# Attention and MLP on one core: where the projection steps, the shared tiles and the pauses stand in a hand-written order

## The chip, the core and the metric

One core of a Trainium2 chip runs the whole kernel. The metric is the device time of one execution in microseconds (us); the number compared is the median over several runs. TensorE is called PE (its weight loads PEld), VectorE DVE, ScalarE ACT, GpSimd POOL, SyncE SP.

## The reference

Eight batches, eight heads, 576 positions, head size 64. Attention keeps only scores within tau of each row's maximum; its output, 4608 rows of 512, goes through two dense layers with g = h - tanh(h) between them.

```python
scores = scale * np.matmul(q, k.transpose(0, 1, 3, 2))
thresh = np.max(scores, axis=-1, keepdims=True) - tau
scores = np.where(scores >= thresh, scores, -1000000000.0)
scores = scores - np.max(scores, axis=-1, keepdims=True)
attn = np.exp(scores)
attn = attn / (np.sum(attn, axis=-1, keepdims=True) + 1e-09)
attn_out = np.matmul(attn, v)
...
x = attn_out.transpose(0, 2, 1, 3).reshape(B * S, H * D)
h = x @ w_in            # 512 -> 2048
g = h - np.tanh(h)
out = g @ w_out         # 2048 -> 512
```

## The kernel before

The order of all instructions is written out by hand; no scheduler moves them. Every engine works through its own instructions in that order and waits only for what it needs.

**Tiles.** Two heads of one batch make a pair; there are 32 pairs p, four per batch. The 576 query rows of two heads are nine tiles of 128 rows: four of each head, and one shared tile that holds the last 64 rows of both. `place(i)` puts the shared tile last in an even pair and first in an odd pair, so the shared tiles of pairs 0 and 1, 2 and 3 and so on are neighbours in the list of 288 tiles. `kind(i)` is "A" for even and "B" for odd tile numbers; an A and the B behind it share some work (one `nb`, one transpose, one attention output).

**One tile.** `scores` multiplies q with the high and low parts of k into a PSUM tile psS of the pool ps_big, which has two buffers: four matmuls on line L331 for a whole tile (512, 64, 512 and 64 columns), eight matmuls with 64 output rows each on line L322 for a shared tile. DVE takes psS out to sc with the row maximum (L341). `shift` makes the bias nb (L353), `kink` lets ACT make z (L368), and z is transposed: by PE (L387) in pairs 0 to 5, by a DMA that SP issues (zT, L375) in the later pairs. `weights` lets ACT take the exponential pT (L396 or L404). `attend` multiplies pT with v (L425, L432, L443), `norm` divides, and `emit_x` transposes a finished pair into xT through psX in the pool ps_h.

**The loop.** Step s of the main loop issues the scores of tile s + 8, z of tile s + 5, the exponential of tile s, and attention of tile s - 2 (in the first 36 tiles the last two come earlier). It also runs what `plan` has for it: loads, the split of q and k on POOL, and `turn`, which transposes k (and some q) on PE through a ps_big buffer, copies it out on DVE (L263) and swaps its halves on POOL (kS, L269). For pairs from 5 on, `turn` of k comes in step 9p - 14 for odd p and 9p - 11 for even p. In one step the order is: shift, scores, kink, tanh of earlier hidden steps, weights, projection and hidden steps, shrink, stores, attend, plan.

**The dense layers.** Stage m handles 512 rows of batch m (the rest of all batches is stage 8). `layers(m)` gives a list of steps of two kinds. A hidden step is four 512-column matmuls into psH of the pool ps_h (L498, two buffers, shared with psX); ACT takes tanh (L511) and DVE makes g (L517) in the next loop step. A projection step is a quarter of a 128-row output: four 512-column matmuls into psY (L524; one buffer, pool ps_y). The fourth quarter is copied out by DVE to yo (L537) and stored by SP (L540). A stage has 16 hidden steps and 16 projection steps. Since a projection needs g, only the first `EARLY(m)` projection steps of block m are in its own stage; the others come in stage m + 1, mixed with that stage's hidden steps. In stage 0 projection waits for all 16 hidden steps.

Stage m starts at step 36(m + 1) + 4, when its x is there. `share` is the number of steps handed out per loop step: the list is spread over 32 loop steps and is finished four steps before the next stage starts. So in each 36 steps there are four without dense work. Stage 7 starts after the last tile and, with stage 8, makes up the tail.

Of the kernel before, what the change touches and what calls it, by code (L numbers as in the profile page):

```python
# [18 lines left out]
def kernel(  # L19
# [14 lines left out]
    B, H, S, D = q.shape  # L34
# [11 lines left out]
    HPAIR = H // 2  # L46
    NPAIR = B * HPAIR
# [4 lines left out]
    TPP = 9  # L52
    NTILE = NPAIR * TPP
# [9 lines left out]
    AHEAD = 8  # L63
    LDK = 16
    MASK = 5
    LAG = 2
# [177 lines left out]
    def q_by_dma(p):  # L244

        return p >= 2 * HPAIR and p % 4 != 0
# [51 lines left out]
    def kind(i):  # L298

        return "AB"[i % 2]  # L300

    def place(i):

        p, j = divmod(i, TPP)
        j = j - p % 2
        return (p, None, 4) if j in (-1, 8) else (p, j // 4, j % 4)

    def scores(i):
        p, hh, t = place(i)
        qT, kT, kS = mats[p, "q"], mats[p, "k"], mats[p, "ks"]  # L310
        ps = ps_big.tile([P, 1024], F32, name="psS", tag="big")
        main, rem, lo = slice(0, 512), slice(512, 576), 0
        if kind(i) == "B":
            main, rem, lo = slice(512, 1024), slice(448, 512), 448
        if hh is None:
            qrem = REM
            if q_by_dma(p):
                qrem = (slice(512, 640, 2), slice(513, 640, 2))
            for n, kk in enumerate((kT, kS)):
                for dst, srcs in ((main, MAIN), (rem, REM)):  # L320
                    for hh in range(2):
                        nc.tensor.matmul(  # L322
                            out=ps[64 * hh : 64 * hh + 64, dst],
                            lhsT=qT[:, qrem[hh]], rhs=kk[:, srcs[hh]],
                            start=(n == 0), stop=(n == 1),
                        )
        else:
            lhs = qT[:, (5 * hh + t) * P : (5 * hh + t + 1) * P]
            for n, kk in enumerate((kT, kS)):
                for dst, src in ((main, MAIN[hh]), (rem, REM[hh])):  # L330
                    nc.tensor.matmul(  # L331
                        out=ps[:, dst], lhsT=lhs, rhs=kk[:, src],
                        start=(n == 0), stop=(n == 1),
                    )
        sc = sc_pool.tile([P, S], F32, name="sc")
        if kind(i) == "B":
            mx = mxs[i] = mxs.pop(i - 1)
        else:
            mx = mxs[i] = mx3[i // 2 % len(mx3)]
        c = int(kind(i) == "B")  # L340
        nc.vector.tensor_scalar(  # L341
            out=sc, in0=ps[:, lo : lo + S], scalar1=SC, scalar2=None,
            op0=ALU.mult, op1=ALU.max, accum_out=mx[:, c : c + 1],
        )
        scs[i] = sc
# [148 lines left out]
    def hidden(m, n, ps):  # L494
        if n == 0:
            gs[m] = g_pool.tile([P, DF_C, MB], BF16, name="g")
        for c in range(DM_C):
            nc.tensor.matmul(  # L498
                out=ps, lhsT=w_in_sb[:, c, n * P : (n + 1) * P],
                rhs=xs[m][:, c, :] if m < B else xR[:, c, :, :],  # L500
                start=(c == 0), stop=(c == DM_C - 1),
            )
        halves.append((m, n, ps))
# [3 lines left out]
    def bend():  # L507
        while halves:
            m, n, ps = halves.pop(0)
            th = t_pool.tile([P, MB], F32, name="th")  # L510
            nc.scalar.activation(out=th, in_=ps, func=ACT.Tanh)  # L511
            ths.append((m, n, ps, th))
# [37 lines left out]
                    )  # L550


    EARLY = lambda m: 3 if m else 3
    LAST = 1

    FIRST = 3
# [2 lines left out]
    def layers(m, tail):  # L559


        def h_step(n):
            if tail and n % 2:
                ps = ps_big.tile([P, MB], F32, name="psHt", tag="big")
            else:
                ps = ps_h.tile([P, MB], F32, name="psH", tag="h")
            hidden(m, n, ps)

        def y_step(m, ms, part):
            if part == 0:  # L570

                odd = tail and (m, ms) > (B - 2, 1) and ms % 2 == 0
                pl, tag = (ps_o, "o") if odd else (ps_y, "y")
                ys[m, ms] = pl.tile([P, d_model], F32, name="psY", tag=tag), odd
            ps, odd = ys[m, ms]
            project(m, ms, part, ps, odd)

        def y_half(h):

            n = d_model // 2  # L580
            pl, tag = ((ps_y, "y"), (ps_o, "o"))[h]
            ps = pl.tile([P, n], F32, name="psY", tag=tag)
            for part in range(4):
                project(m, 3, part, ps, h == 0, slice(h * n, h * n + n))

        now = quarters(m - 1)[EARLY(m - 1) :] if m > 0 else []
        if m < NMB - 1:
            now += quarters(m)[: EARLY(m)]
        else:
            now += quarters(m)[:12]  # L590
        n = 16 + len(now)


        ahead = n - max(0, EARLY(m) - 3) - LAST if m < NMB - 1 else n - 9 - LAST
        steps, at, i = [], [], 0

        def ready(y):
            last = 4 * y[2] + 3
            return y[0] < m or len(at) > (last if m else 15) and at[last] + 2 < i

        while now or len(at) < 16:
            if len(at) < 16 and (
                not now or not ready(now[0]) or len(at) * ahead <= i * 16
            ) and not (m == B - 1 and i < FIRST):
                steps.append(lambda a=len(at): h_step(a))
                at.append(i)
            elif ready(now[0]):
                steps.append(lambda y=now.pop(0): y_step(*y))
            else:
                steps.append(lambda: None)  # L610
            i += 1
        if m == NMB - 1:
            steps += [lambda h=h: y_half(h) for h in range(2)]
        return steps
# [15 lines left out]
    def w_cast():  # L630
        flat, wt, i, cols = loaded.pop(0)
        nc.gpsimd.tensor_copy(out=flat[:, i * cols : (i + 1) * cols], in_=wt)
# [26 lines left out]
    for p in range(1, NPAIR):  # L659
        first = TPP * p - AHEAD  # L660
        for d, f in PREP[3 if p == 1 else 0 :]:
            d -= p == 1 and d in (3, 5)
            if d in (7, 8) and q_by_dma(p):
                d = d + 2
            if p in (2, 4):
                d = {8: 9, 7: 8, 5: 6}.get(d, d)
            elif d == 5 and p >= 5:
                d = 6 if p % 2 else 3
            plan.setdefault(first - d, []).append(lambda p=p, f=f: f(p))
        d = 7 if q_by_dma(p) else 3 - (p == 1 or p >= 5)  # L670
        d = 4 if p in (2, 4) else d
# [16 lines left out]
    todo, stage = [], 0  # L688
# [4 lines left out]
            plan.setdefault(-AHEAD, []).extend(plan.pop(at))  # L693


    kinks, wts, atts = {}, {}, {}
    for i in range(NTILE + 3):
        at = i - 4 if i < HPAIR * TPP else i
# [4 lines left out]
    for s in range(-AHEAD, NTILE + LAG + 3):  # L703
        p, j = divmod(max(s, 0), TPP)
        if 0 <= s < NTILE and j == 2 + LAG and p % HPAIR == 0 and p >= HPAIR:
            assert not todo
            todo = layers(stage, False)
            share = len(todo) / (HPAIR * TPP - 2 - LAG)
            done, stage = 0.0, stage + 1
        if s == NTILE:  # L710
            todo = layers(stage, True)
            share, done, stage = 1, 0.0, stage + 1
        if 0 <= s + AHEAD - 1 < NTILE:
            shift(s + AHEAD - 1)
        if 0 <= s + AHEAD < NTILE:
            scores(s + AHEAD)
        if s == 1 - AHEAD:
            for t in ("k", "q", "ks"):
                turn_first(t, 1)
        for i in kinks.pop(s, []):  # L720
            kink(i)
        bend()
        for i in wts.pop(s, []):
            weights(i)
        if 0 <= s < NTILE + FIRST:
            if todo:
                done += share
                if s < NTILE and j == TPP - 1 and p % HPAIR == HPAIR - 1:
                    done = 1e9
                while todo and done >= 1:  # L730
                    todo.pop(0)()
                    done -= 1
        if s == 0:
            nc.vector.tensor_tensor(
                out=fold, in0=ident_bf[:, 0:64], in1=ident_bf[:, 64:P], op=ALU.add
            )
        shrink()
        for store in stores[:-1]:
            store()
        del stores[:-1]  # L740
        for i in atts.pop(s, []):
            pp, jj = divmod(i, TPP)
            if i < NTILE:
                attend(i)
                odd = pp % 2
                if jj == 3 + odd:
                    norm(pp, 0)
                elif odd and jj in (0, 8):
                    norm(pp - (jj == 0), 1)
            if pp and jj == 1 + pp % 2:  # L750
                emit_x(pp - 1)
        for step in plan.pop(s, []):
            step()
        if s + AHEAD in cast_when:
            w_cast()
        if s + AHEAD in load_when:
            w_load(next(pieces))
# [54 lines left out]
```

## Time and profile before

| | |
|---|---|
| median of five runs | 533.52 us (532.0 to 535.44) |
| the profiled execution | 532.75 us, span 530.9 us |
| granted TensorE clock | 0.998 |
| busy, share of the span | PE 96%, ACT 82%, DVE 79%, POOL 55%, PEld 54% |
| PE instructions | 4606 matmuls, 4606 weight loads |
| projection matmuls (L524) | 592, 145.9 us |
| hidden matmuls (L498, into psH) | 480, 123.3 us |
| score matmuls of whole tiles (L331), with kT and with kS | 512 and 496, 104.4 and 101.3 us |
| eviction of scores (L341, DVE) | 288, mean 752 ns |
| exponential of a pair of tiles (L404, ACT) | 117, mean 1154 ns |

The chain of work that ended last is PE for 44% of the span, "issue" 16%, POOL 15%, ACT 11% and DVE 8%. Times of groups are busy times; a matmul's end is modelled, and neighbours overlap. "Idle before" is time in which the engine stood still just ahead of a group, with what ended it. The steps of the loop can be found in the trace by counting psS tiles: those of step s are tile s + 8.

### The profile page before, as it was taken

The page shows a single profiled execution, that of the slowest core. Times are in us where ns is not written, and L with a number is a line of the kernel's source. Part 1 is how long each engine was busy: PE and PEld are TensorE (multiplying, and loading weights), DVE is VectorE, ACT ScalarE, POOL GpSimd, SP SyncE. Part 2 cuts the span into 40 slices and gives each one's busy share as a digit, 9 for nine tenths or more (in the row PEclk, how much of TensorE's full clock was granted, in tenths as well). Part 3 has the DMA queues.
Part 4 walks back from the last instruction along what each step waited for, and adds up shares of the span by engine and source line. Part 5 has one row for each costly group of instructions (what it writes and reads, how often), then busy time and mean ns, then how long its engine had stood idle before and what let it go on. Part 6 is the DMA issues. An engine that isn't in the chain of part 4 may idle for free.

```text
span 530.9 us, 12716 instructions
## 1 busy us (share of the span) xinstructions
PE 507.8 (96%) x4606; PEld 287.5 (54%) x4606; DVE 420.9 (79%) x1179; ACT 434.6 (82%) x617; POOL 289.9 (55%) x390
## 2 busy tenths in 40 slices
PE   8999899988999999999999999999999999999996
PEld 4666566554555555555555555655555555444444
DVE  5899879997889988898889988898889887554440
ACT  5999899979898979899898989898989999544330
POOL 7999989684736657575727574665757530000000
PEclk9999999999999999999999999999999999999999
DMA  7843659989988999799998999899999996400113
GB/s 204 255 139 111 215 187 189 169 151 203 177 205 160 182 183 214 168 184 211 171 199 179 199 180 203 172 189 197 203 173 182 205 146 110 105 36 26 38 41 80
DMA packets 208607, 86.79 MB, mean 163 GB/s; under 512 B 176160, under 2 KB 200992, under 8 KB 208544
## 3 DMA queue, kind: packets, MB, share of 16 engines
q1 hardware_dynamic: 207952, 85.56, 76.1%
q8 instruction: 36, 0.59, 0.5%
q10 hardware_dynamic: 592, 0.43, 0.3%
q14 instruction: 27, 0.22, 0.1%
HBM read 36.70 MB, written 9.44 MB: 87 GB/s over the span
## 4 chain that ended last, share of the span: by engine, by line
PE 44%; issue 16%; POOL 15%; ACT 11%; DVE 8%; DMA 4%; SPq 1%; POOLq 0%; ACTq 0%; DVEq 0%
PE psY L524 14%; PE psH L498 11%; PE psS L331 8%; ACT z L368 5%; POOL kS L269 5%; ACT pT L396 3%; DMA zT<-z 3%; DVE sc L341 3%; PE psHt L498 3%; PE psO L432 2%; POOL khl L193 2%; ACT pT L404 2%; PE psS L322 2%; ACT th L511 2%; DVE g L517 2%
## 5 line engine op out<-in xcount | busy, mean ns | idle before, releaser
L341 DVE TENSOR_SCALAR_CACHE_REDUCE sc<-psS 128x576 f32<-128x576 f32 x288 | 214.0, 752 | 38.2 <-PE psS L331 24.9
L368 ACT ACTIVATE z<-sc,nb 128x576 bf16<-128x576 f32 x288 | 215.4, 769 | 19.8 <-DVE nb L353 17.9
L404 ACT ACTIVATE pT<-zT 128x1152 f16<-128x1152 bf16 x117 | 135.0, 1154 | 15.9 <-DMA zT<-z 15.9
L524 PE MATMUL psY<-w_out_sb,g 128*128 128x512 bf16 (+1 forms) x592 | 145.9, 373 | 0.8 <-DVE yo L537 0.8
L269 POOL COPY kS<-kT 64x1152 f16<-64x1152 f16 x62 | 70.9, 1143 | 122.0 <-DVE nb L353 120.4
L498 PE MATMUL psH<-xT,w_in_sb 128*128 128x512 bf16 x480 | 123.3, 379 | 3.5 <-DVE g L517 3.5
L331 PEld LDWEIGHTS <-qT 128*128 128x128 f16 x1024 | 74.5, 97 | 61.7 <-issue 7.5
L331 PE MATMUL psS<-kT,qT 128*128 128x512 f16 (+1 forms) x512 | 104.4, 285 | 3.2 <-DVE sc L341 1.5
L517 DVE SCALAR_TENSOR_TENSOR g<-th,psH 128x512 bf16<-128x512 f32 x128 | 87.5, 684 | 21.3 <-ACT th L511 20.9
L331 PE MATMUL psS<-kS,qT 128*128 128x512 f16 x496 | 101.3, 286 | 1.9 <-POOL kS L269 1.9
L511 ACT ACTIVATE th<-psH 128x512 f32<-128x512 f32 x128 | 74.7, 584 | 22.3 <-PE psH L498 21.8
L524 PEld LDWEIGHTS <-g 128*128 128x128 bf16 x592 | 51.0, 98 | 56.8 <-issue 2.4
L498 PEld LDWEIGHTS <-w_in_sb 128*128 128x128 bf16 x576 | 49.3, 98 | 58.5 <-issue 6.0
L432 PE MATMUL psO<-vb,pT 128*128 128x65 bf16 x1024 | 53.3, 194 | 0.0
L432 PEld LDWEIGHTS <-pT 128*128 128x128 f16 x1024 | 44.2, 98 | 9.7
L193 POOL TENSOR_TENSOR qhl<-qraw,qhl 128x576 f16<-128x576 f32 x31 | 39.7, 1281 | 2.6
L193 POOL TENSOR_TENSOR khl<-kraw,khl 128x576 f16<-128x576 f32 x31 | 39.7, 1280 | 2.6
L396 ACT ACTIVATE pT<-psZ 128x512 f16<-128x512 bf16 (+1 forms) x54 | 35.1, 654 | 3.3 <-PE psZ L387 3.1
L537 DVE COPY yo<-psY 128x512 f32<-128x512 f32 (+1 forms) x31 | 21.1, 682 | 14.1 <-PE psY L524 12.4
L425 PE MATMUL psO<-vb,pT 128*128 128x130 bf16 x128 | 28.2, 221 | 3.4 <-ACT pT L404 2.7
L458 DVE TENSOR_TENSOR osb<-psO,rc 128x256 bf16<-128x256 f32 x64 | 27.2, 424 | 2.2
L263 DVE COPY kT<-ps_k 128x1152 f16<-128x1152 f16 x31 | 23.3, 751 | 3.9 <-PE ps_k L240 3.9
(79 smaller groups left out, 508.9 us busy)
## 6 DMA issues: line engine op xcount, KB each, us to landing
vraw<-in_v_dram SPq DMA_DIRECT2D x32, 256.0 KB, 4.0
out_dram<-yo SPq DMA_DIRECT2D x32, 256.0 KB, 2.8
kraw<-in_k_dram SPq DMA_DIRECT2D x31, 256.0 KB, 3.4
qraw<-in_q_dram SPq DMA_DIRECT2D x31, 256.0 KB, 3.5
wt<-in_moe_w_in_dram SPq DMA_DIRECT2D x8, 512.0 KB, 4.9
wt<-in_moe_w_out_dram SPq DMA_DIRECT2D x8, 512.0 KB, 4.0
zT<-z SPq DMA_TRANSPOSE x117, 3.6
qraw<-in_q_dram SPq DMA_DIRECT2D x32, 32.0 KB, 3.5
```

The lines of the kernel that those rows point to most:

```text
L193: nc.gpsimd.tensor_tensor(out=hl[:, :, 1, :], in0=x, in1=hl[:, :, 0, :], op=ALU.subtract)
L269: nc.gpsimd.tensor_copy(out=o, in_=i)
L331: nc.tensor.matmul(out=ps[:, dst], lhsT=lhs, rhs=kk[:, src], start=(n == 0), stop=(n == 1),)
L341: nc.vector.tensor_scalar(out=sc, in0=ps[:, lo : lo + S], scalar1=SC, scalar2=None, op0=ALU.mult, op1=ALU.max, accum_out=mx[:, c : c + 1],)
L368: nc.scalar.activation(out=z, in_=sc, func=ACT.Prelu, bias=nb, scale=1.0, alpha=STEEP)
L396: nc.scalar.activation(out=pt[:, off * P : (off + n) * P], in_=ps[:, 0 : n * P], func=ACT.Exp)
L404: nc.scalar.activation(out=pt[:, 0 : n * P], in_=zts.pop(i)[:, 0:n, :], func=ACT.Exp)
L432: nc.tensor.matmul(out=po[:, t - 1 + ab, :], lhsT=pt[:, blk * P : (blk + 1) * P], rhs=vb[:, hh, c, :], start=False, stop=(n == 7), skip_gr ...
L498: nc.tensor.matmul(out=ps, lhsT=w_in_sb[:, c, n * P : (n + 1) * P], rhs=xs[m][:, c, :] if m < B else xR[:, c, :, :], start=(c == 0), stop= ...
L511: nc.scalar.activation(out=th, in_=ps, func=ACT.Tanh)
L517: nc.vector.scalar_tensor_tensor(out=gs[m][:, n, :], in0=th, scalar=-1.0, in1=ps, op0=ALU.mult, op1=ALU.add,)
L524: nc.tensor.matmul(out=ps, lhsT=gs[m][:, n, ms * P : (ms + 1) * P], rhs=w_out_sb[:, n, cols], start=(n == 0), stop=(n == DF_C - 1),)
```

## The change

Four things are changed, all of them in the order of the instructions; PE's instructions are the same 4606 matmuls as before, in another order.

- `EARLY(m)` is max(3, 9 - m) instead of 3. Stage 0 has 16 hidden and 9 projection steps (before 16 and 3), stages 1 to 6 have 16 and 15 (before 16 and 16), stages 7 and 8 are as before.
- In `layers`, `ahead` follows `EARLY`: hidden steps come earlier in their stage, and in stage 0 one with each step until all 16 are out.
- The list of a stage is spread over all steps up to the start of the next stage, except those in which `turn` of a k is planned (`turns`). Stage 6, the last one within the tiles, is spread over its last 32 loop steps as before.
- The scores of a shared tile of kind A are held back by one step and issued right ahead of those of the shared tile of kind B.

```diff
-    EARLY = lambda m: 3 if m else 3
+    EARLY = lambda m: max(3, 9 - m)
...
         ahead = n - max(0, EARLY(m) - 3) - LAST if m < NMB - 1 else n - 9 - LAST
+        if m == 0:
+            ahead = 16
...
+    turns = set()
+    for p in range(HPAIR + 1, NPAIR):
+        d = 6 if p % 2 else 3
+        turns.add(TPP * p - AHEAD - (d if p >= 5 else 5))
...
-            share = len(todo) / (HPAIR * TPP - 2 - LAG)
+            room = range(s, min(s + HPAIR * TPP, NTILE))
+            if room[-1] + 1 < NTILE:
+                room = [a for a in room if a not in turns]
+            share = len(todo) / len(room)
...
-        if 0 <= s + AHEAD < NTILE:
-            scores(s + AHEAD)
+        n = s + AHEAD
+        if 0 < n < NTILE and place(n)[1] is None and kind(n) == "B":
+            scores(n - 1)
+        if 0 <= n < NTILE and (place(n)[1] is not None or kind(n) == "B"):
+            scores(n)
...
-            if todo:
+            if todo and (s >= NTILE or s in room):
                 done += share
-                if s < NTILE and j == TPP - 1 and p % HPAIR == HPAIR - 1:
+                if s < NTILE and s == room[-1]:
```

## The prediction

> **What bounds the kernel now.** I read the page's busy shares and its 40 slices first, then busy time stage by stage, then the order of time on TensorE, then the waits.
>
> ```profile
> PE 507.8 (96%) x4606; PEld 287.5 (54%) x4606; DVE 420.9 (79%) x1179; ACT 434.6 (82%) x617; POOL 289.9 (55%) x390
> ...
> PE   8999899988999999999999999999999999999996
> DMA  7843659989988999799998999899999996400113
> ```
>
> PE is at nine tenths or more nearly everywhere from the tenth slice on; a shared average would hide that the first quarter is different. So I cut the span where the hidden layer of each block starts (matmul psS of step s = 40, 76, 112, ..., 256):
>
> ```profile
> core 0: us, PE busy (x) PEld busy (x) DVE busy (x) ACT busy (x) POOL busy (x), PEclk, DMA share, GB/s
> 65.06:121.52 56.46, 51.21 (x550) 31.65 (x548) 48.57 (x141) 50.66 (x77) 46.50 (x58) 1.00 0.83 180
> 121.52:179.15 57.63, 56.70 (x521) 31.73 (x519) 50.00 (x142) 52.01 (x72) 33.46 (x44) 1.00 0.93 184
> 352.81:410.00 57.19, 56.39 (x522) 31.67 (x520) 50.29 (x144) 52.01 (x72) 34.43 (x45) 1.00 0.96 190
> 410.00:447.73 37.73, 37.10 (x325) 20.17 (x323) 32.69 (x93) 34.95 (x49) 12.81 (x17) 1.00 0.85 155
> ```
>
> The first row is stage 0, the next ones stage 1, stage 5 and the start of stage 6. Stages 1 to 5 take 57.63, 58.23, 57.76, 57.67 and 57.19 us, 288.48 together. A PE matmul's end is modelled, so I count starts instead: in the trace a 512-column matmul follows the last after 0.216 us, a 65-column one after 0.03 us, a transpose after 0.055 us. Time beyond such distances is PE standing still: 2.0, 2.6, 2.2, 2.1 and 1.6 us in stages 1 to 5 (10.4 in all), 7.4 in stage 0, 1.0 from 410.00 to 447.73. So stages 1 to 5 are 55.6 us of PE work each and PE is their bound; ACT, next, has 52 us. Stage 0 has only 56.46 - 7.4 = 49.1 us of PE work: it isn't bound by PE, and PE's largest halt lies there:
>
> ```profile
> 111.95 0.42 PE L432 MATMUL psO<-vb,pT 128*128 128x65 bf16 x8
> 112.21 0.41 PE L331 MATMUL psS<-kT,qT 128*128 128x512 f16 x2
> ...
> 117.88 0.41 PE L331 MATMUL psS<-kS,qT 128*128 128x512 f16 x2
> 120.95 0.23 PE L425 MATMUL psO<-vb,pT 128*128 128x130 bf16 x1 [2.66 <-ACT pT L404]
> ```
>
> In the four tiles without projection before s = 76, PE runs ahead and then waits 2.66 us for an exponential. The same tiles of a later stage:
>
> ```profile
> 175.84 0.41 PE L322 MATMUL psS<-kS,qT 128*64 128x512 f16 x4
> 176.08 0.42 PE L322 MATMUL psS<-kT,qT 128*64 128x512 f16 x4
> ...
> 177.35 0.41 PE L331 MATMUL psS<-kS,qT 128*128 128x512 f16 x2
> 177.79 0.41 PE L331 MATMUL psS<-kT,qT 128*128 128x512 f16 x2
> 178.03 0.41 PE L331 MATMUL psS<-kS,qT 128*128 128x512 f16 x2
> 178.58 0.23 PE L425 MATMUL psO<-vb,pT 128*128 128x130 bf16 x1
> ```
>
> 0.44 and 0.55 where 0.24 would do, and a third such place: 0.6 us of standing per stage, since evictions and exponentials can't follow at 0.9 us a tile.
>
> **Part 1, nine projection steps in stage 0.** Six steps leave stages 1 to 6, one each, and join stage 0. A step is four matmuls; the lines below give 144.78 - 143.92 = 0.86 us. Stages 1 to 5 lose 5 x 0.86 = 4.3 us, stage 6 0.86. Stage 0 gains 5.2 us of PE work: 49.1 + 5.2 = 54.3, above ACT's 50.66, so it turns PE-bound. With the standing of a PE-bound stage (1.6 to 2.6) it would take 56 to 57; with all 7.4 kept, 61.7. I take 3.1, nearer the PE-bound rows because the 2.66 us halt is in the very tiles that now get four projection steps (3.4 us): 57.4, so +0.9 (bounds -0.5 and +5.2). The moved steps also bring two yo copies (0.69 us of DVE each) and two stores into stage 0; DVE has 48.57 of 56.46 there; a store's issue takes SP some 0.55 us, ahead of the zT issues queued behind it, which land up to 4 us before ACT wants them. I count both at nothing; uncovered, the copies would cost 1.4 us and the issues 1.1. All 16 hidden steps of stage 0 now come in s = 41 to 63 (14 there before): 2 x 0.58 of tanh and 2 x 0.68 of g move earlier, inside the +0.9.
>
> **Part 2, joined shared tiles.** A shared tile uses matmuls of 64 output rows (L322):
>
> ```profile
> 143.92 1.03 PE L524 MATMUL psY<-w_out_sb,g 128*128 128x512 bf16 x4
> 144.78 0.22 PE L425 MATMUL psO<-vb,pT 128*128 128x130 bf16 x1
> 144.84 0.41 PE L432 MATMUL psO<-vb,pT 128*128 128x65 bf16 x8
> 145.18 0.44 PE L322 MATMUL psS<-kT,qT 128*64 128x512 f16 x4
> 145.45 0.42 PE L322 MATMUL psS<-kS,qT 128*64 128x512 f16 x4
> 145.80 1.04 PE L498 MATMUL psH<-xT,w_in_sb 128*128 128x512 bf16 x4
> ```
>
> Eight 65-column matmuls take 0.34 us before an L322 (144.84 to 145.18) and 0.26 before an L331 (111.95 to 112.21); the last L322 before a full one takes 0.35 (145.45 to 145.80), before another L322 0.24 (175.84 to 176.08). A visit thus costs 0.08 + 0.11 = 0.19 us. In the order of PE's instructions there are 25 visits before and 16 after. Where two shared tiles fell in tiles without projection they already stood together; so the nine that go are three before s = 40, where ACT sets the pace (56.49 of 65.06 us busy; I count 0, at most 0.6), and one in each of stages 1 to 6: 5 x 0.19 = 1.0 and 0.2. The joined step puts two evictions (752 ns each) in a row on DVE; behind them wait yo and the g of the step before, 0.75 us later. The score buffers are two and both were freed a step earlier, and the step before has no eviction; I count 0.
>
> **Part 3, even spread.** Steps now fill the four empty tiles, and each stage's four steps that transpose a k (turn) get none. The 0.6 us per stage in the empty tiles goes: 3.0 over stages 1 to 5. What is late next: ps_h has two buffers, and a hidden step needs the g of the one before last. Where a psX lies between two hidden steps in neighbouring tiles, that g comes only after this step's eviction, 0.75 + 0.68 us. By the schedule's order this happens twice, at s = 58 and 94 (bounds 0 and 1.5 each; I take 1.1 for s = 94, and s = 58 is in stage 0's +0.9); before, milder forms of it stood three times a stage. Together I put the standing of stages 1 to 5 at 8.5 instead of 10.4: -1.9 (bounds -6.4, 0.8 a stage, and 0).
>
> One rule of the Trainium skill speaks against parts 1 and 3: Perfetto Trace Analysis, Identifying the Most-Contended Engine, holds busy matmul time to be a bad measure for TensorE and asks for the weight loads' share, which is 54% here. By it TensorE has room to spare, moving its work would shorten nothing, and the sum would be 0. The starts, 216 ns apart with 2 us of standing in 57.7, decide against it here.
>
> **Sum.** Stages 1 to 5: -4.3 - 1.0 - 1.9 = -7.2; stage 6: -1.05; stage 0: +0.9; before s = 40 and after 447.73 (same steps): 0. That is -7.3. The profiled execution took 532.75 (its span is 530.9), so 525.4 on its scale; the median of the runs is 0.77 above it: 533.5 - 7.3 = 526.2.
>
> **Rivals.** (a) *Stage 0 does not hide the steps.* Its halts come from latencies (exponentials, g) that the new work only pushes on: +5.2 instead of +0.9, so -3.0: 530.5. For it: ACT and DVE are also at 50.7 and 48.6 there. Against it: 2.66 of 7.4 us is one halt that the steps fill.
>
> (b) *The transposes by DMA hold the stages.*
>
> ```profile
> ACT pT L404 <- DMA zT<-z: 11.9, 8, 2.4
> ```
>
> From 121.52 to 410 ACT waits 11.9 us for zT, and DMA is at 0.93 to 0.96. If that paces the stages they can't get below the shortest one: 5 x 57.19 - 288.48 = -2.5; stage 6 gives nothing, stage 0 +0.9: -1.6, so 531.9. Against it: these waits hardly reach PE (2.2 us for pT in the same stretch), and even spacing takes away the bursts that cause some of them.
>
> (c) *Slower: the turn steps lose their cover.* There are 24 (four in each of stages 0 to 5). PE needs 2.71 us for one with a projection and psX (s = 85), 1.85 without it; DVE's eviction, g, xT, xR and kT copy take 2.4 by their starts. Where no psX lies, 1.3 against 1.95. If the next scores wait for the kT copy every time, that is 24 x 0.6 = 14.4 us: 533.5 - 7.3 + 14.4 = 540.6. It decides from (7.3 + 2.7) / 24 = 0.42 us a turn step. Against it: DVE has only 50.4 of 57.7 us, the next step gives it 1.65 us for one eviction, and the second buffer gives the copy one more step.
>
> (d) That the change doesn't do what it says is excluded: the order shows 16 visits, and nine projection steps before the next stage's first hidden step.
>
> **Numbers.** Forecast 0.70; (a) 0.12; (b) 0.11; (c) 0.07. The forecast's own range: down by 4.5 (standing), 1.4 (stage 0) and 0.6, not all at once: 520.5; up by 1.9 and 1.6: 529.7. With (a), and (b) up to its centre: 520.5 to 532.0; (c), half of (b) and the tails are left out. About 0.5% (2.7 us) is what a measurement of this kernel can tell from no change. Faster: nearly all of the forecast and half of (a), 0.75; same: most of (b), half of (a), 0.16; slower 0.09.
>
> **What would show it.** Right: stages 1 to 5 near 56.2 each; stage 0 near 57.4 with no halt of over 1 us before s = 76; 16 visits of L322; PE standing near 1.7 a stage. (a): stage 0 over 60. (b): stages over 57 with ACT waiting for zT. (c): PE standing for kT or sc in the step behind each turn. The prediction is wrong if stages 1 to 5 stay above 57.5, or fall below 55.

## The result and the profile after

The changed kernel takes 532.33 us (median of 46 runs, 530.94 to 535.96), the kernel before 533.69 (86 runs). The ratio is 0.9978, interval 0.997 to 0.9987: 1.2 us faster, where 7.3 were forecast. It lies just above the range's upper end of 532.0.

The profiled execution took 533.72 us, with a span of 531.9. That is 1.4 above the median of its kernel, while the one of before was 0.9 below its own; the two executions therefore differ by +1.0 where the medians differ by -1.4. So whatever rests on a difference of 1 us between two profiles is shown by timed kernels below, not by the profiles alone.

The busy shares on the changed kernel's page:

```profile
PE 507.7 (95%) x4606; PEld 286.2 (54%) x4606; DVE 419.0 (79%) x1179; ACT 434.7 (82%) x617; POOL 289.3 (54%) x390
```

Nothing has moved here, and nothing could: the work is the same. Busy time by stage, cut at the same loop steps as before (length first, then the engines):

```profile
64.56:122.40 57.84, 55.53 (x574) 33.58 (x572) 50.39 (x143) 51.24 (x77) 47.89 (x60) 1.00 0.81 179
122.40:181.90 59.50, 56.64 (x518) 31.34 (x515) 49.87 (x143) 53.83 (x73) 34.41 (x45) 1.00 0.94 186
...
355.27:411.68 56.41, 55.58 (x517) 31.20 (x515) 49.06 (x143) 50.69 (x69) 34.33 (x44) 1.00 0.97 185
411.68:448.29 36.61, 36.17 (x320) 19.80 (x318) 31.76 (x93) 33.89 (x47) 10.90 (x13) 1.00 0.90 156
```

Stage 0 is 57.84 (forecast 57.4), the start of stage 6 is 1.12 shorter (forecast 1.05). Stages 1 to 5 are 59.50, 57.15, 57.49, 58.73 and 56.41: 289.3 together, where 281.3 were forecast and 288.5 stood before. PE's work in them, by the distances of the starts, is 272.5 instead of 278.05: the forecast 5 x (0.86 + 0.19) = 5.25 is there. What isn't there is the time: PE stands still for 16.8 us instead of 10.4. By the matmul that stood still:

| stages 1 to 5, us | before | changed |
|---|---|---|
| scores (psS) in the 3 us behind a turn, and the turn itself (ps_k) | 0.9 | 8.0 |
| projection, waiting for yo (psY) | 0 | 2.1 |
| psX, waiting for g | 0 | 1.75 |
| hidden step, waiting for g (psH) | 4.1 | 1.8 |
| scores elsewhere, attention (psO) | 3.05 | 1.0 |
| second half of the scores, waiting for kS | 2.4 | 2.2 |

Of the 8.0 us, 4.6 stand within 1 us of a turn: 3.5 at the ten turns of even pairs, 1.1 at the ten of odd pairs, whose steps also hold a psX. Before the change these were 0.

A turn step of an even pair in the changed kernel, PE in the order of time (start, duration, operation, idle time before it), and below it the two evictions of DVE in the same stretch:

```profile
243.42 0.41 PE L331 MATMUL psS<-kT,qT 128*128 128x512 f16 x2
243.67 0.41 PE L331 MATMUL psS<-kS,qT 128*128 128x512 f16 x2
243.94 0.22 PE L425 MATMUL psO<-vb,pT 128*128 128x130 bf16 x1
244.00 0.41 PE L432 MATMUL psO<-vb,pT 128*128 128x65 bf16 x8
244.59 0.66 PE L240 MATMUL ps_k<-ident_f,khl 128*128 128x128 f16 x9 [0.18 <-DVE sc L341]
245.26 0.41 PE L331 MATMUL psS<-kT,qT 128*128 128x512 f16 x2
```

```profile
243.78 0.75 DVE L341 TENSOR_SCALAR_CACHE_REDUCE sc<-psS 128x576 f32<-128x576 f32 x1
...
244.45 0.75 DVE L341 TENSOR_SCALAR_CACHE_REDUCE sc<-psS 128x576 f32<-128x576 f32 x1
```

The transposes begin 0.59 us after the 65-column matmuls where 0.26 would do, and the next scores 0.67 after the transposes where 9 x 0.055 = 0.5 would do. Both wait for sc: they start 0.06 us after the first and the second eviction have ended (244.53 and 245.20). ps_big has two buffers, and turn takes one: between these scores and the next ones that want the same buffer PE now has only the attention and the transposes, about 0.8 us, and DVE needs 0.75 for the eviction alone, behind whatever it was doing. A dense step of 0.86 us used to stand between them. The prediction's 1.3 us of PE work where no psX lies is there (1.84 from 243.42 to 245.26, less 0.5 of standing); its hope for "one more step" was not fulfilled, since the wait is for the eviction too, not only for the copy of kT. PE standing for sc at the turns is also the sign that the prediction had named for its rival (c).

### The profile page after: what moved, and what is told of

Read it like the earlier page. It is cut to its first block, busy times and chain, and to the rows that moved or that the text cites. A ratio compares the mean times of both kernels' runs of the same rounds, so it can differ in the third digit from the quotient of the medians.

```text
span 531.9 us, 12676 instructions
## 1 busy us (share of the span) xinstructions
PE 507.7 (95%) x4606; PEld 286.2 (54%) x4606; DVE 419.0 (79%) x1179; ACT 434.7 (82%) x617; POOL 289.3 (54%) x390
## 4 chain that ended last, share of the span: by engine, by line
PE 43%; DVE 14%; issue 12%; ACT 11%; POOL 9%; DMA 9%; SPq 0%; ACTq 0%; POOLq 0%; DVEq 0%
PE psY L524 13%; PE psH L498 12%; PE psS L331 9%; DMA zT<-z 7%; DVE sc L341 5%; ACT z L368 4%; DVE g L517 3%; POOL kS L269 3%; ACT pT L396 3%; PE psHt L498 3%; ACT pT L404 2%; PE psO L432 2%; ACT th L511 2%; DMA vraw<-in_v_dram 2%; DVE kT L263 1%
## 5 line engine op out<-in xcount | busy, mean ns | idle before, releaser
L368 ACT ACTIVATE z<-sc,nb 128x576 bf16<-128x576 f32 x288 | 218.5, 769 | 21.3 <-DVE nb L353 20.5
```

What stands on the lines that cost most here:

```text
L368: nc.scalar.activation(out=z, in_=sc, func=ACT.Prelu, bias=nb, scale=1.0, alpha=STEEP)
```

## The experiments

Seventeen kernels, all timed beside the kernel before (533 to 534 us in each set; 0.5% is 2.7 us). Kernels of different sets are compared by their medians; by their ratios to the kernel before, a difference can come out up to 1.4 us apart, so where the two disagree both are given. Where a profile lacks some matmul records (62 to 68 of 4606), the distance that a missing one leaves is not counted as standing.

**Fill the turn steps.** The one line that keeps them empty goes:

```diff
             room = range(s, min(s + HPAIR * TPP, NTILE))
-            if room[-1] + 1 < NTILE:
-                room = [a for a in room if a not in turns]
```

> The change, but the turn steps get dense steps too (spread over all 36 loop steps of a stage). Theory 1 (uncovered turns): in the changed kernel PE stands 8.0 us in stages 1 to 5 between a turn and the scores behind it, or ahead of the turn, against 0.9 before; with a dense step in front of each turn that falls to 2 at most and the time to 526 to 528 us. Theory 2 (the denser hidden steps make DVE late everywhere): the standing moves to other places and the time stays within 531 to 534.

Measured: 526.05, ratio 0.9845 (0.9819 to 0.9871). This is the time that the prediction gave for the change. A turn step of that kernel:

```profile
240.41 0.41 PE L331 MATMUL psS<-kS,qT 128*128 128x512 f16 x2
240.65 1.03 PE L498 MATMUL psH<-xT,w_in_sb 128*128 128x512 bf16 x4
241.52 0.22 PE L425 MATMUL psO<-vb,pT 128*128 128x130 bf16 x1
241.57 0.41 PE L432 MATMUL psO<-vb,pT 128*128 128x65 bf16 x8
241.83 0.66 PE L240 MATMUL ps_k<-ident_f,khl 128*128 128x128 f16 x9
242.38 0.41 PE L331 MATMUL psS<-kT,qT 128*128 128x512 f16 x2
```

0.26 and 0.55: no halt. The standing at the turns of stages 1 to 5 falls from 8.0 to 2.9 (2 at most were expected), all standing there from 16.8 to 11.1. Theory 1 holds for this kernel, theory 2 doesn't.

**The old spread, and each part alone.**

```diff
-            room = range(s, min(s + HPAIR * TPP, NTILE))  # and without turns
+            room = range(s, s + HPAIR * TPP - 2 - LAG)
```

> The change with the old spread (32 loop steps in a row, four empty ones), so early projection steps and joined shared tiles alone. Theory 1: PE work of stages 1 to 6 falls by 1.05 us each, standing stays as before, stage 0 grows by 1.4: 533.7 - 6.3 + 1.4 = 528.8, range 528 to 530.5. Theory 2: the hidden steps come as densely as in the change, so 532 or more.

Measured: 534.02, ratio 1.0008 (0.9992 to 1.0024). A miss for theory 1, and within what theory 2 said.

> The kernel before with the early projection steps alone. Theory 1: 6 x 0.86 us less work in stages 1 to 6, stage 0 longer by 1.4: 533.7 - 3.8 = 529.9, range 529 to 531.5. Theory 2: 533 or more. Rival (a) of the prediction: stage 0 grows by all 5.2, so 533.7.

Measured: 535.0, ratio 1.0026 (1.0008 to 1.0043). The early steps alone make the kernel slower, as theory 2 said. Stage 0 takes 59.43 us, 3.0 more than before, and its largest halt is one that the prediction never looked for (PE in the order of time):

```profile
107.92 0.60 PE L524 MATMUL psY<-w_out_sb,g 128*128 128x512 bf16 x2
109.97 0.59 PE L524 MATMUL psY<-w_out_sb,g 128*128 128x512 bf16 x2 [1.45 <-POOL w_out_sb L634]
```

The first projection steps overtake POOL's cast of w_out. In the changed kernel projection begins at 105.3 us instead of 100.9, and this halt isn't seen. PE's work in stages 1 to 5 fell by 4.3 as computed; standing rose from 10.4 to 13.6.

> The kernel before with the even spread alone (turn steps and no others left empty). Theory 1: some 7 us of standing at the turns of stages 1 to 5 come in, 2 to 3 us in the four empty tiles of each stage go: 536 to 539. Theory 2: with the old sparse hidden steps the spread costs nothing and saves the empty tiles' standing: 530 to 533.

Measured: 534.99, ratio 1.0022 (1.0006 to 1.0039). Slower, by less than theory 1 said; neither range was met. PE stands 7.9 us at the turns of stages 1 to 5 instead of 0.9, and most of the standing at empty tiles and psH went.

So the early steps alone and the spread alone each cost a little over 1 us, the early steps with the joined tiles in the old spread change nothing that can be told from noise, and the three together gain 1.2 us. The joined tiles alone were not run.

**Which part does the filled kernel need?**

> The change with dense steps in the turn steps too, but without the joined shared tiles. By 0.19 us for a visit: with dense steps between them none of the neighbouring shared tiles of stages 0 to 6 stands together any more, so 13 joints take a second visit, 2.5 us: 528 to 529 against 526.05 of the kernel with the join. Rival: the join's double eviction costs as much as the visits save: 526.

Measured: 525.98, ratio 0.9855 (0.983 to 0.9881): no difference, the rival's number. In its profile PE works 2.1 us more in stages 1 to 5, as the further visits ask, and stands 7.6 us instead of 11.1; that it is the double evictions which cost this was not tested by itself.

> The change with dense steps in the turn steps too, but with three early projection steps in every stage as before. If the early steps are worth what the sum said once the turns are covered (6 x 0.86 less work, stage 0 longer by 1.4): 526.05 + 3.8 = 529.9, range 529 to 531. Rival: they are worth nothing, as in the kernel with the early steps alone, and the gain is all the spread's: 525 to 527.

Measured: 526.33, ratio 0.9863 (0.9839 to 0.9888): no difference either.

> The kernel before with its dense steps spread over all 36 loop steps of a stage, and nothing else changed. If the early steps and the joined tiles are worth nothing once there are no empty steps, as the two runs without one of them say: 525.5 to 527. If each of them only covers for the other: 528 to 530.

Measured: 528.78, ratio 0.9919 (0.9901 to 0.9938). Both together are worth 2.7 us by the medians, 3.9 by the ratios (the intervals don't meet); a spread without empty steps is worth 4.2 by itself. Beside the spread with empty turn steps alone (534.99) that is 6.2 us: the empty turn steps have the same price here as in the changed kernel (532.33 against 526.05).

> Dense steps in the turn steps too, and six yo copies on ACT in place of DVE: those after which the next dense step opens psY again at once. PE stood 2.1 us in stages 1 to 5 and 0.45 in stage 0 for these copies in the filled kernel. If ACT is free there (no tanh is left in these steps): 524 to 525. Rival: ACT is late itself and the exponentials behind the copy are pushed on by 0.6 us each: 526 or more.

Measured: 527.1, ratio 0.9879 (0.9855 to 0.9902): no gain, the rival's number. The halts for yo were not cured but grew: in its profile psY stands 3.7 us in stages 1 to 5 instead of 2.1, and 2.4 in stage 0, where the longest halt is for ACT's copy. Whether late exponentials add to it was not looked into.

**Does it matter where the empty steps are?**

```diff
-        turns.add(TPP * p - AHEAD - (d if p >= 5 else 5))
+        turns.add(TPP * p - AHEAD - (d if p >= 5 else 5) + 4)
```

> The change, but the four empty steps of a stage stand four steps behind each turn of k instead of in it. Theory 1 (the turn step needs a dense step in front of the turn): the 8.0 us of standing go and 526 to 528 is reached as in the filled kernel. Theory 2 (31 dense steps in 32 places instead of 36 are too close together, wherever the gaps are): 531 to 533.

Measured: 531.92, ratio 0.9968 (0.9946 to 0.999). A miss for theory 1 as it stood, and within theory 2's range: the standing at the turns did go (8.0 to 1.7), but 5.2 us ahead of psX came in its place. In this one execution the longest of these halts (2.05 us) is followed by 3.4 us at a granted clock of 0.50, with matmuls twice as far apart; other runs at a clock of 1.0 took up to 533.45, so the clock is not what keeps this kernel slow.

> The change with only two empty steps in a stage, those of the turns of odd pairs. If every empty step costs the same wherever it stands (6.3 us for 24 of them, 0.26 us each): 12 steps, 529.2. If the cost comes from the turns of even pairs, where 0.2 to 0.5 us of standing was seen at nearly each of them: 527.

Measured: 526.85, ratio 0.9886 (0.9864 to 0.9907). With empty steps at the odd pairs' turns alone most of the cost is gone: by the medians 0.8 of 6.3 us is left, by the ratios 2.2 of 7.1. Half would have been left if each empty step cost the same, a ratio of 0.9911 and just outside the interval. It fits the trace of the changed kernel, where the halts next to a turn lie at the even pairs (3.5 us against 1.1).

**The second cause: SP's queue.** Where did the 5.2 us ahead of psX come from? A milder form of the same wait stands in the filled kernel (first the order of time on ACT, then on SP, whose rows are DMA issues, then a row of DVE and one of PE):

```profile
294.98 0.76 ACT L368 ACTIVATE z<-sc,nb 128x576 bf16<-128x576 f32 x1
...
304.43 1.17 ACT L404 ACTIVATE pT<-zT 128x1152 f16<-128x1152 bf16 x1 [1.81 <-DMA zT<-z]
305.50 0.76 ACT L368 ACTIVATE z<-sc,nb 128x576 bf16<-128x576 f32 x1
306.17 0.57 ACT L511 ACTIVATE th<-psH 128x512 f32<-128x512 f32 x1
```

```profile
295.63 1.57 SPq L375 DMA_TRANSPOSE zT<-z  x1
297.24 0.61 SPq L145 DMA_DIRECT2D qraw<-in_q_dram  x1
297.90 0.57 SPq L153 DMA_DIRECT2D qraw<-in_q_dram  x1
298.51 0.59 SPq L145 DMA_DIRECT2D vraw<-in_v_dram  x1
299.14 1.73 SPq L151 DMA_DIRECT2D vraw<-in_v_dram  x1
300.97 2.76 SPq L375 DMA_TRANSPOSE zT<-z  x2
```

```profile
306.78 0.69 DVE L517 SCALAR_TENSOR_TENSOR g<-th,psH 128x512 bf16<-128x512 f32 x1 [1.25 <-ACT th L511]
```

```profile
307.52 0.38 PE L475 MATMUL psX<-ident_bf,osb 128*128 128x128 bf16 x4 [1.23 <-DVE g L517]
```

The z of one pair of tiles was ready at 295.74, but SP issued its transpose only at 300.97, behind another transpose and four loads. ACT stood 1.81 us for it; behind that stood a tanh, behind the tanh a g, and behind the g PE, 1.4 us ahead of psX by the starts. SP issues without a pause from 295.63 to 303.73. For these 8 us the trace is the second case in the Trainium skill's Perfetto Trace Analysis, What "DMA-bound" means: an issuing engine's track that is solid with DMA slices. It is so in bursts only: in stages 1 to 5 of this kernel SP waits 117 us for ACT. The remedy that the page names for this case, large descriptors, was not tried; the loads were set apart instead:

```diff
-        (LDK - 1, lambda p: load(p, "q")),
-        (LDK - 2, lambda p: load(p, "v")),
+        (LDK - 2, lambda p: load(p, "q")),
+        (LDK - 5, lambda p: load(p, "v")),
```

> All three parts, no empty steps, and the loads of q and v of a pair set one and three steps later, so that SP doesn't issue four loads between two transposes. Theory D (SP's queue and the DMA behind it hold the exponentials now; ACT waited 10.6 us for zT in stages 1 to 5 of the filled kernel, one z lay 5.2 us before SP came to it): the wait falls below 6 us and the time to 523 to 525. Rival (these waits are absorbed before they reach PE): 526, whatever ACT waits.

Measured: 521.84, ratio 0.9788 (0.9769 to 0.9807). The fastest kernel of the study, 11 us under the kernel before and below what was expected. In the waits of the whole span, first of the filled kernel, then of this one (total, times, longest):

```profile
ACT pT L404 <- DMA zT<-z: 15.0, 17, 2.3
```

```profile
ACT pT L404 <- DMA zT<-z: 3.5, 8, 0.8
```

PE's standing in stages 1 to 5 is 7.1 us. The DMA share there is 1.01, not lower than in the changed kernel (0.94 to 1.00), so the order in the queue changed and not the load on the DMA engines.

> As the kernel with the loads set apart, but with three early projection steps in every stage. Theory D: with SP out of the way PE is the bound again, so the early steps are worth 2 to 4 us: 526 to 528 here. Rival: still worth nothing, within 1 us of the kernel with them.

Measured: 523.36, ratio 0.9817 (0.9798 to 0.9836). The early steps are worth 1.5 us here, less than expected. The intervals of the two ratios overlap, but the kernels were timed side by side, and each run of this one (522.9 to 523.6) is above each run with the early steps (521.4 to 522.1). Stages 2 to 5 of its profile take 55.65, 55.65, 55.75 and 55.65 us: PE-bound, with 0.3 to 0.4 us of standing.

> The kernel before, with nothing but these loads set later. Theory D: most of the 4.1 us that PE stood for psH in stages 1 to 5 came from late exponentials, so 529 to 531. Rival: PE had the cover for it, 532 to 533.5.

Measured: 529.46, ratio 0.9933 (0.9917 to 0.9948). The kernel before gains 3.6 us from this alone. The number is theory D's, the place is not: psH in stages 1 to 5 falls only from 4.1 to 2.4, and these stages together by 1.2 us (288.48 to 287.24). The larger part is stage 0, which falls from 56.46 to 53.86: the 2.66 us halt, which the prediction gave to the empty tiles and meant to fill with projection, is gone without any projection. In the profile before, the z behind that halt was ready at 111.02, its transpose was issued at 114.53, behind a transpose of q and four loads, and landed 5.1 us later.

> The kernel before with these loads set later and with the early projection steps, old spread. If SP's queue is what ate the early steps' gain: 2 to 4 us under the same kernel without the early steps. If the four empty steps ate it (psX, psY and the exponentials behind the empty steps): as slow as that kernel or slower.

Measured: 531.83, ratio 0.9973 (0.9963 to 0.9983), 2.4 us slower than without the early steps. In the old spread it isn't SP that ate them: stage 0 grows from 53.86 to 59.43, 5.6 us, as much as was moved into it; 1.5 of this is the wait for POOL's cast of w_out again.

> The changed kernel, empty turn steps and all, with the loads of q and v set one and three steps later. Theory 1 and D side by side (the turns' standing has to do with the score buffers, not with SP): it keeps the turns' 8 us and gains only what SP held, 528 to 530. If the empty steps hurt through SP's queue: 522 to 524, as with no empty steps.

Measured: 528.26, ratio 0.9908 (0.9894 to 0.9923). The changed kernel gains 4 us when its loads are set apart, and still stands 5.4 us at the turns of stages 1 to 5. It is 6.4 us behind the filled one with the same loads, so the price of the empty turn steps (6.3 and 6.2 above) doesn't come from SP's queue.

> The change with its empty steps four steps behind the turns, and the loads of q and v set later. With empty steps there the standing at the turns was gone (1.7 us), but 5.2 us stood ahead of psX, behind tanh that waited for late zT. If those were SP's doing, they go and this kernel beats the one with empty turn steps (528.26): 524.5 to 526.5. If an empty step costs the same anywhere: 528.

Measured: 526.33, ratio 0.9853 (0.9827 to 0.9879). The standing ahead of psX falls from 5.2 to 1.0, so most of it was SP's doing, and the kernel is now under the one with empty turn steps, by ratios of 0.9853 and 0.9908 whose intervals don't meet. The turn step is a worse place for an empty step than another; empty steps elsewhere still cost, 526.33 against 521.84. What these 4.5 us consist of was not found; that the dense steps stand closer together, theory 2 of this place, remains possible.

> The fastest kernel so far (no empty steps, loads set later) without the joined shared tiles. With SP out of the way PE is the bound, so 13 further visits of the half-width form at 0.19 us come in full: 523.5 to 525. Rival: the joined steps' two evictions cost as much elsewhere: 521.8 again.

Measured: 522.65, ratio 0.9786 (0.9763 to 0.9808): the joined tiles' gain can't be told from nothing here.

Taken together, with the loads as they were, every kernel with four empty steps in a stage took 532 to 535 us, wherever they stood, and every kernel without any 526 to 529. With the loads set apart it is 526 to 532 and 522 to 523.

## Why the prediction was wrong, point by point

- **What bounds stages 1 to 5.** Right as far as PE's starts go: in the profiles with all matmul records PE's work was found again within 0.3 us a stage. But a stage bound by PE at 96% isn't bound by PE alone once 1 us of its work is taken. The weight loads' share, by which the rule that the prediction set aside would judge, is 54 to 55% in kernels from 535 to 522 us; it doesn't tell them apart.
- **Part 1.** Stage 0 was sized well in the changed kernel (57.84 for 57.4), and stage 6 too. The reason was half wrong: the halt to be filled came from loads ahead of a transpose in SP's queue (stage 0 is 53.86 without it), and with that out of the way stage 0 grows in the old spread by all of the moved work. That is rival (a)'s size, though 1.5 of the 5.6 us is a wait that it did not name. In the even spread with the loads apart stage 0 grows by 1.0 (55.55 to 56.56), as forecast. The two yo copies, counted at nothing, cost 0.6 us at psY in stage 0 of the changed kernel; in stages 1 to 5, where no cost of psY's one buffer had been counted either, they cost 2.1. The Trainium skill says this in Perfetto Trace Analysis, Optimizing Tensor Performance, Matmuls: independent groups should rotate through PSUM banks. Six times in the changed kernel a fourth quarter is followed by the next first quarter; before, never.
- **Part 2.** The count of visits was right, 25 to 16, and so was their PE time. As a gain it can't be shown: 526.05 with and 525.98 without, 521.84 with and 522.65 without.
- **Part 3 is the step that failed.** Its term for the even spread was -1.9 and came out at +6.4 between the two profiles (10.4 to 16.8), which themselves differ by 2.4 us more than the medians. Timed alone, the spread costs 1.3 us. The 0.6 us a stage at the empty tiles did go, and the halts for psH halved. But the turn steps, left empty, priced at 0.6 us each under rival (c) and then counted at 0, came in at 8.0 / 20 = 0.40 each, 0.36 above what stood there before. The mechanism was written down with its place and its price, and set aside on DVE's average load of 87% over a stage, when the question was what DVE does in 0.8 us. By the prediction's own sum 7.3 / 24 = 0.30 a step would have used up the gain, and 0.42 would have made the kernel clearly slower. The timed kernels give less than the profile: filling the 24 steps brings 6.3 us, 0.26 each, and 7.3 - 6.3 = 1.0 is about the gain that was left. Not all of this is the eviction's: empty steps four steps behind the turns cost 4.5 us where those in the turns cost 6.4 (loads apart), so that the place accounts for some 2 us, and why the rest is lost stays open.
- **Rival (b)** was set aside because ACT's waits for zT "hardly reach PE". In the place shown they reach PE by way of tanh, g and psX, where PE's wait names DVE. Setting the loads apart took 3.0 to 5.6 us off each of seven kernels by the medians (2.5 to 6.1 by the ratios).
- **The sum** would have been right for the kernel with no empty steps, 526.05 for 526.2, but not by its terms: what that kernel gains is mostly the spread's, and its early steps and joined tiles are worth 2.7 us together (3.9 by the ratios) where 5 x 0.86 + 0.86 + 1.2 = 6.4 were counted, less stage 0's 0.9. That the number fits is luck.
- **Open.** Why the early steps and the joined tiles can each be taken from the filled kernel at no cost while both together cost 2.7 us. What makes empty steps cost 4.5 us away from the turns. What holds stage 1, which takes 56 to 60 us in every kernel. Loads on another queue than SP's were not tried.

## What to carry to other kernels

Before work is taken out of a step to make it "even", look at what that step covers: with two buffers, the time between a producer's two visits to the same buffer has to hold one eviction, and an average load says nothing about it. When a wait chain ends at the bound engine, follow it back past the engine that it names; here DVE was named, and four loads ahead in SP's queue were the cause. A gap that seems to invite work should first be removed by its cause: the halt in stage 0 vanished when two loads were set later.

## What the runs showed of the hardware

A load's issue holds SP's queue for some 0.6 us (0.57 to 1.73 in the rows above), and that of a transpose of 128 x 1152 for 1.4 in the median of all profiles (1.57 above); one transpose and four loads in a row put 5.2 us between a finished z and its transpose. A full-array matmul next to a half-width one starts 0.08 to 0.11 us later than next to another full one, and PE's 512-column matmuls follow each other at 0.216 us in all kernels, so PE's work can be added up from starts to within 0.3 us in a stage, in the six profiles with all records and their six orders of it.
